# A linear-attention and state-space block on one core: chunk 14, the last v product and the passage to the output stage in another order, and slope rows padded to 64

## The chip, the core and the metric

The kernel runs on one core of one Trainium2 chip. The time is device microseconds (us) of one execution; the figure of a kernel is the median of its runs. One execution was also recorded by the hardware profiler, and all rows below come from it. The core's engines are TensorE (PE, with its weight loads as PEld), VectorE (DVE), ScalarE (ACT), GpSimd (POOL) and SyncE (SP, which here issues the DMAs). Each runs its own instructions in the order of the program and waits on semaphores of the others.

## The reference

Two branches over S = 2048 positions and D = 448 channels, mixed by a gate (shortened):

```python
g = sigmoid((x * gate_w).sum(-1, keepdims=True))
q, k, v = heads(x @ wqkv)                     # 16 heads of 28
phi = lambda t: where(t > 0, t + 1, exp(t)) + 1e-6
kv  = einsum("bhsd,bhse->bhde", phi(k), v);  z = phi(k).sum(s)
a   = (phi(q) @ kv) / (phi(q) . z + 1e-6) @ wo
K   = 2 Re sum_n C[d,n] exp(A[d,n] dt[d] l)   # kernel of the state-space branch, l = 0..L-1
b   = causal_conv(u, K) + u * D_skip
out = g * a + (1 - g) * b
```

## The kernel before

The positions are 16 chunks of 128. All products run on PE, single-precision data split into a rounded high part and a low part, so that a product takes three passes or so (names in h and l).

**The chunk loop** (`c` from 1 to 14) works on several chunks at once. In its turn c, PE computes k of chunk c+1 (`project`, tile `k`), the v products of chunks behind (`do_v`: `tri` times the scaled input, for the convolution's short part), q of chunk c (tile `q`), and adds chunk c to `g` (`do_g`), four banks that gather phi(k) against x. ACT and DVE make the features: `k_exp`, `k_max`, `k_high` (`pkh`), `k_low` (`pkl`), `k_sum` (adds phi(k) to `zb`), and likewise `q_exp`, `q_max`, `q_add` for `pq`. POOL takes low parts of x and the skip term. `v_post` scales the v product, `v_add` adds it to `y`, `v_row` sends its last row by DMA into `u`.

**The passage.** After the last k, `zb` is split into `zh` and `zl`, summed over partitions by a product with ones (tile `zo`, name `k`) and copied back to `zb`. `z_products` multiplies the rows of `u` by `ru` and sends `u` and `ru` by four DMAs into `zr`; `zst` is `zr` split into a high and a low part. `gate` and `gates_a` make the gate values of chunks 0 to 13, `gates_b` transposes them into `phs`, and `phi` sends these by DMA into `rows`. The banks of `g` are copied to `gs`, multiplied by `wv` (`kv_products`), masked and split into `kvz` (`kv_split`, `kv_again`), and multiplied by `wo` (split into `woh`, `wol`, in tiles `wos`) to `mh` and `ml` (`mrows`, products `m`). `inter(0)` and `inter(1)` multiply `gcat` by `zst` (products `z`) into `rc`, the carried state for chunks 0 to 7 and 8 to 15.

**The output stage** runs over c from 0 to 15. For each chunk: `norm_a` (POOL, `prod` = pq times zb), `norm_b` and `norm_d` (DVE, `den`: sums by head, plus 1e-6, times the gate's factor, reciprocal), `norm_c` (POOL, `pn` = pq times den), `norm_e` (ACT, copies 64 columns of `pn`), `turn` (PE, four transposes `tr`; then `th` on ACT and its low part on DVE), `tail` (ACT, gate rows into the low part), `attend` (PE, eleven products `a`), `final_b` (DVE, adds `y`, and the DMA out) and `final_c` (ACT). Each of these is issued some chunks ahead of `attend`. A generator `late` finishes q of chunk 15 and `inter(1)` within this loop.

**What sets the order.** The scheduling is manual: each engine executes in the order in which the code calls the helpers, so moving a call moves its instructions on their engine's queue. Tiles come from pools with a fixed number of buffers; a new tile waits until the readers of the old one are done. In the passage the helpers `z_products` (L539), `gates_b`, `turn`, `inter` and the calls from L634 to L927 are what the change touches.

Of the kernel before, what the change touches and what calls it, by code (L numbers as in the profile page):

```python
# [179 lines left out]
def gated_mix_kernel(ctx: ExitStack, tc: tile.TileContext, xin, wv_d, wo_d, abc_d, ldt_d, dsk_d,  # L180
# [82 lines left out]
    def low(eng, o, r, h):  # L263
        eng.tensor_tensor(out=o, in0=r, in1=h.bitcast(F32), op=ALU.subtract)  # L264
# [272 lines left out]
    U = slice(0, NC - 1)  # L537

    def z_products():  # L539
        zr = tp.tile([P, D], F32, name="zr", tag="w")[:64]  # L540
        POOL.memset(zr, 0.0)
        DVE.tensor_tensor(out=ru[U], in0=u[U], in1=ru[U], op=ALU.mult)
        for o in (0, 32):
            for k, w in enumerate((u[U], ru[U])):
                SP.dma_start(out=zr[o + k * (NC - 1):o + (k + 1) * (NC - 1)], in_=w)
        return zr
# [60 lines left out]
        q_max(n)  # L607
    do_g(0)
    woh, wol = [], []
    for c in range(1, NC - 1):  # L610
        if c == 1:
            load_x(4)
            gcr = tp.tile([P, D], F32, name="gcr", tag="w")[:KZ, :2 * RX].rearrange("p (g m) -> p g m", g=2)
            for o, i in ((mask, mask_d), (gcr, gcat_d), (sel, sel_d)):
                SP.dma_start(out=o, in_=i)
        elif c + 3 < NC:
            load_x(c + 3)
        if c == 4:
            SP.dma_start(out=wv, in_=wv_d)
            SP.dma_start(out=wo, in_=wo_d)  # L620
        ko, k_run = pieces(c + 1, wkh, wkl, D, "v0" if c in (2, 4) else "k")
        k_run(KA)
        if c == LAG + 2:
            steps(1)
        k_run(11)

        def split_next():
            if c + 2 < NC:
                split_x(c + 2)
                low(POOL, xl[c + 2], xr[c + 2][:, :NAT], xh[c + 2][:, :NAT])  # L630
# [36 lines left out]
        if c == 1:
            for n in range(2):
                q_add(n)
            steps(1)  # L670
        for n in now[1:]:
            v_post(n)
        if c == NC - 2:
            gate(0, NC - 2)
            g2 = gates_a(1, NC - 2)
        k_low(c + 1)
        k_sum(c + 1)
        for n in now[1:]:
            v_add(n)
        if c == NC - 2:  # L680
            zh = tp.tile([P, D], F32R, name="zh", tag="e")
            zl = tp.tile([P, D], F32R, name="zl", tag="t")
            ACT.copy(zh, zb)
            low(DVE, zl, zb, zh)
            zr = z_products()
        if c < NC - 2:
            vq = [vs.pop(0) for _ in range(1 + (c + 1 in TWICE))] if c > LAG + 1 else []
        if LAG + 2 < c < NC - 2:
# [12 lines left out]
        if LAG + 1 < c < NC - 2:  # L701
            for n in vq:
                do_w2(n)
        for n in now:
            v_row(n)
        if c > 1:
            q_add(c)
        drip(c, 2)
        if c in (NC - 6, NC - 4):
            wos = xs.tile([DJ, 2, 2, D], F32R, name="wos", tag="x")  # L710
            woh.append(wos[:, 0])
            wol.append(wos[:, 1])
            ACT.copy(woh[-1], wo[:, 2 * len(woh) - 2:2 * len(woh)])
        if c == NC - 6:
            low(POOL, wol[0], wo[:, 0:2], woh[0])
        if c < NC - 2:
            do_g(c)
        if c == LAG:
            POOL.tensor_copy(gcat, gcr)
# [33 lines left out]
    def norm_e(c):  # L753
        ACT.copy(pn[c][:, D:], pn[c][:, EV:D])
# [109 lines left out]
    v_post(vq[0])
    low(DVE, wol[1], wo[:, 2:4], woh[1])
    zo = ps.tile([P, 512], F32, name="k", tag="k")
    do_g(NC - 2, (0, 1, 2))
    PE.matmul(zo[:1, D:D + 1], lhsT=ones[:DJ, :1], rhs=oks, start=True, stop=True)
    PE.matmul(zo[:, :D], lhsT=ones_r, rhs=zh, start=True, stop=False)
    PE.matmul(zo[:, :D], lhsT=ones_r, rhs=zl, start=False, stop=True)  # L870
    ACT.copy(zb, zo[:, :D])  # L871
    DVE.tensor_copy(okn, zo[:1, D:D + 1])
# [126 lines left out]
def _layout(inputs):  # L999
# [79 lines left out]
```

## Time and profile before

| | |
|---|---|
| median of 3 runs | 183.65 us (183.55 to 183.81) |
| the profiled execution | 183.66 us, its span 181.9 us |
| PE, PEld | 175.4 us (96%), 155.1 us (85%) |
| DVE, ACT, POOL | 134.7 us (74%), 119.1 us (65%), 97.0 us (53%) |
| granted TensorE clock | 1.000 |

The span is from the first to the last instruction. The busy time of an engine is the union of its instructions; matmuls overlap each other, so PE's share says that it had work, and PE's waits show as distances between starts. In rows of the time order the columns are start, length (both us), engine, line, operation, tiles written and read, shape and count; in brackets stands how long the engine sat idle before it and who ended that. The loop's last turn (14) takes PE from about 111 to 118 us, the passage runs from there to 134 us, and the output stage from there to the end.

### The profile page before, as it was taken

To read this page: it belongs to the slowest core of one execution; us is meant where nothing else is said; L and a number is where in the kernel's file an instruction comes from. 1 tells how busy PE (TensorE), PEld (TensorE's weight loads), DVE (VectorE), ACT (ScalarE), POOL (GpSimd) and SP (SyncE) were. 2 spreads that over 40 slices of the span, in tenths; PEclk is the share of its full clock that TensorE was granted. 3 is DMA by queue.
4 is the path that set the end of the run, shared out by engine and by line. 5 is a ranking of instruction groups with operands and counts; after the bars stand their busy time and mean duration, and the time that the engine had idled before them with its cause. 6 is when DMAs were issued, how large, how long until landed. Compare 5 with 4: busy or idle time off the path is not lost.

```text
span 181.9 us, 2800 instructions
## 1 busy us (share of the span) xinstructions
PE 175.4 (96%) x896; PEld 155.1 (85%) x896; DVE 134.7 (74%) x265; ACT 119.1 (65%) x257; POOL 97.0 (53%) x90
## 2 busy tenths in 40 slices
PE   7999999999999999999999999999999999999991
PEld 7699999998988888898887999879887899889990
DVE  0876288765977799888978878577999698977530
ACT  3979596684755667666687676483665766765631
POOL 1059979651096437155284738039857857874000
PEclk9999999999999999999999999999999999999999
DMA  5999960960021302303032100000001212212212
GB/s 184 368 334 314 302 221 15 392 205 4 0 67 49 116 14 102 115 5 116 9 109 66 58 0 1 6 15 8 2 1 51 106 51 102 97 56 109 101 78 86
DMA packets 8356, 18.34 MB, mean 101 GB/s; under 512 B 1772, under 2 KB 5568, under 8 KB 8112
## 3 DMA queue, kind: packets, MB, share of 16 engines
q1 hardware_dynamic: 8192, 17.88, 28.9%
q10 hardware_dynamic: 144, 0.23, 0.4%
q8 instruction: 9, 0.15, 0.3%
q14 instruction: 11, 0.09, 0.2%
HBM read 14.25 MB, written 3.67 MB: 99 GB/s over the span
## 4 chain that ended last, share of the span: by engine, by line
PE 59%; DVE 15%; issue 11%; ACT 6%; POOL 5%; DMA 2%; POOLq 0%; ACTq 0%
PE a L800 16%; PE g L490 11%; PE q L391 10%; PE k L391 9%; PE tr L778 3%; PE v L391 2%; PE v L506 2%; PE v L556 2%; DVE den L734 2%; DMA xr<-in 2%; DVE v L497 2%; ACT xw L271 2%; POOL xw L264 1%; DVE th L783 1%; DVE wkl L264 1%
## 5 line engine op out<-in xcount | busy, mean ns | idle before, releaser
L264 POOL TENSOR_TENSOR xw<-xr,xw 128x448 fp32r<-128x448 f32 (+1 forms) x28 | 34.5, 1252 | 37.5 <-ACT xw L271 28.0
L490 PE MATMUL g<-pkh,xw 128*128 128x448 f32 x112 | 35.5, 366 | 0.0
L391 PE MATMUL q<-wqh,xw 128*128 128x450 f32 x112 | 32.4, 369 | 0.0
L391 PE MATMUL k<-wkh,xw 128*128 128x448 f32 x96 | 27.6, 369 | 0.0
L800 PE MATMUL a<-wkh,th 128*128 128x448 f32 (+1 forms) x119 | 26.9, 365 | 0.0
L729 POOL TENSOR_TENSOR prod<-pq,zb 128x448 f32<-128x448 f32 x16 | 19.2, 1204 | 10.9 <-ACT zb L871 8.3
L490 PE MATMUL g<-pkl,xw 128*128 128x448 f32 x64 | 23.5, 367 | 0.0
L490 PEld LDWEIGHTS g<-pkh,xw 128*128 128x128 f32 x112 | 21.1, 188 | 2.6
L391 PEld LDWEIGHTS q<-wqh,xw 128*128 128x128 f32 x112 | 21.0, 188 | 1.8
L800 PEld LDWEIGHTS a<-wkh,th 128*128 128x128 f32 x119 | 20.7, 191 | 1.2
L750 POOL TENSOR_TENSOR pn<-pq,den 128x448 f32<-128x448 f32 x16 | 15.5, 969 | 8.7 <-DVE den L741 4.4
L391 PEld LDWEIGHTS k<-wkh,xw 128*128 128x128 f32 x96 | 18.0, 188 | 2.0 <-issue 0.3
L278 POOL TENSOR_TENSOR y<-xr,rows 128x448 f32<-128x448 f32 x15 | 17.5, 1166 | 0.0
L391 PE MATMUL q<-wql,xw 128*128 128x450 f32 x42 | 15.4, 368 | 0.0
L805 DVE SCALAR_TENSOR_TENSOR ot<-y,og,a 128x448 f32<-128x448 f32 (+1 forms) x17 | 10.5, 618 | 6.4 <-PE a L800 6.4
L458 ACT ACTIVATE pq<-q 128x448 f32<-128x448 f32 x13 | 7.1, 544 | 12.2 <-DVE q L454 11.0
L412 DVE SCALAR_TENSOR_TENSOR k<-k,e 128x448 f32<-128x448 f32 x13 | 8.2, 632 | 9.0 <-ACT e L409 9.0
L271 ACT CAST xw<-xr 128x1024 fp32r<-128x1024 f32 x13 | 13.6, 1042 | 1.7 <-PE v L506 1.7
L782 ACT CAST th<-tr 128x512 fp32r<-128x512 f32 x16 | 9.4, 587 | 8.0 <-PE tr L778 7.7
L783 DVE TENSOR_TENSOR th<-tr,th 128x512 fp32r<-128x512 f32 x16 | 11.0, 689 | 4.3 <-ACT th L782 4.2
L811 ACT COPY pq<-a 128x448 f32<-128x448 f32 (+1 forms) x17 | 8.7, 514 | 6.9 <-DVE ot L805 6.8
L391 PE MATMUL k<-wkl,xw 128*128 128x448 f32 x36 | 13.2, 367 | 0.0
(182 smaller groups left out, 372.8 us busy)
## 6 DMA issues: line engine op xcount, KB each, us to landing
xr<-in SPq DMA_DIRECT2D x13, 512.0 KB, 4.9
out<-ot SPq DMA_DIRECT2D x15, 224.0 KB, 1.9
pq<-in SPq DMA_DIRECT2D x2, 896.0 KB
xr<-in SPq DMA_DIRECT2D x4, 256.0 KB
y<-in SPq DMA_DIRECT2D x4, 225.0 KB
wv<-in SPq DMA_DIRECT2D x1, 896.0 KB
wo<-in SPq DMA_DIRECT2D x1, 784.0 KB
y<-in SPq DMA_DIRECT2D x3, 224.0 KB, 4.3
```

What stands on the lines that cost most here:

```text
L264: eng.tensor_tensor(out=o, in0=r, in1=h.bitcast(F32), op=ALU.subtract)
L271: ACT.copy(h[:, :XC], r)
L278: POOL.tensor_tensor(out=y[:, c], in0=xr[c][:, NAT:LO], in1=dsk, op=ALU.mult)
L391: PE.matmul(o[:, :n], lhsT=a, rhs=b, start=run.n == 1, stop=not seq)
L490: PE.matmul(g[i][:a.shape[1], :D], lhsT=a, rhs=b, start=c == 0 and n == 0, stop=c == NC - 1 and n == len(seq) - 1)
L729: POOL.tensor_tensor(out=pd[c], in0=pq[:, c], in1=zb, op=ALU.mult)
L750: POOL.tensor_tensor(out=hd(n[:, :D]), in0=hd(pq[:, c]), in1=dn[c // 2][:, c % 2, :, None].to_broadcast([P, H, DH]), op=ALU.mult)
L782: ACT.copy(h, ov)
L783: DVE.tensor_tensor(out=l, in0=ov, in1=h.bitcast(F32), op=ALU.subtract)
L800: PE.matmul(a[:, lo:hi], lhsT=u_, rhs=w_[:, lo:hi], start=n == 0, stop=n == 10)
L805: DVE.scalar_tensor_tensor(out=ot[:, lo:hi], in0=y[:, c, lo:hi], scalar=og[:, c:c + 1], in1=a[:, lo:hi], op0=ALU.mult, op1=ALU.add)
L811: ACT.copy(pq[:, c, lo:hi], a[:, lo:hi])
```

## The change

The loop ends after c = 13, and turn 14 is written out behind it, in another order. In it DVE makes `ru` and scales the last v product ahead of the k maximum of chunk 15, the sum `k_sum` comes directly behind the maximum, and the gates come behind `zl`; the copy of `zb` comes ahead of `q_add`. The low parts of `wo` go to POOL, in halves of 448 columns. `zr`, `zst` and `gcat` have 94 rows instead of 62: the low part starts at row 64 instead of 32. POOL makes both parts of `zst`, behind its first two `prod`. Chunk 0 is transposed (`turn(0)`, and `norm_e(0)` before it on ACT) ahead of the rest of q of chunk 15 and of `mrows`. The last `v_add` moves from the passage into `late`, behind `attend(2)`. No instruction's result is dropped.

```diff
-KZ = 32 + NZ
+KZ = 64 + NZ
@@ z_products
-        zr = tp.tile([P, D], F32, name="zr", tag="w")[:64]
+        zr = tp.tile([P, D], F32, name="zr", tag="w")[:KZ]
-        for o in (0, 32):
+        for o in (0, 64):
-    for c in range(1, NC - 1):
+    for c in range(1, NC - 2):
...
-            low(POOL, wol[0], wo[:, 0:2], woh[0])
+            for j in range(2):
+                low(POOL, wol[0][:, j], wo[:, j], woh[0][:, j])
...
+    ko = project(NC - 1, wkh, wkl, D, "k")
+    kvz = xs.tile([DJ, 2, EV + NAT], F32R, name="kvz", tag="x")
+    POOL.memset(kvz.bitcast(F32), 0.0)
+    k_exp(NC - 1, ko)
+    do_v(NC - 1)
+    zr = z_products()
+    v_post(NC - 1)
+    for j in range(2):
+        low(POOL, wol[1][:, j], wo[:, 2 + j], woh[1][:, j])
+    POOL.memset(rows[DT:RX, :RG * P], 0.0)
+    k_max(NC - 1)
+    k_sum(NC - 1)
+    k_high(NC - 1)
...
+    ACT.copy(zh, zb)
+    k_low(NC - 1)
+    low(DVE, zl, zb, zh)
+    q_exp(NC - 2, project(NC - 2, wqh, wql, D + 2, "q"))
+    gate(0, NC - 2)
+    g2 = gates_a(1, NC - 2)
...
+    ACT.copy(zb, zo[:, :D])
+    q_max(NC - 2)
+    q_add(NC - 2)
...
     norm_a(0)
     norm_a(1)
-    POOL.memset(rows[DT:RX, :RG * P], 0.0)
-    do_g(NC - 2, (3,))
+    POOL.tensor_copy(zst, zr)
+    low(POOL, zst[64:], zr[64:], zst[64:])
     norm_bd(0)
     norm_c(0)
...
-            phs_low = gates_b(g2, "pkl")
-    ACT.copy(zst, zr[:KZ])
+            gates_b(g2, "pkl")()
+    norm_bd(1)
+    norm_a(2)
+    norm_c(1)
     norm_a(3)
+    norm_e(0)
...
     kv_again()
-    low(DVE, zst[32:], zr[32:KZ], zst[32:])
-    phs_low()
+    turn(0)
...
     mrows(1, p3, "a")
-    norm_bd(3)
+    norm_d(3, 1)
     norm_a(4)
-    v_add(vq.pop(0))
...
     def late():
         yield 2
+        v_add(c)
         last = inter(1)
```

What this does to the queues is seen at three places. The first is DVE from the k maximum (`k<-k,e`) of chunk 15 to the scaling of the last v product (`t<-v,rows`); `e_60` is the gate's row `e1`, `g_1243` the gate values to be transposed. Before:

```order
L412 SCALAR_TENSOR_TENSOR k<-k,e 128x448
L469 TENSOR_SCALAR e_60<-e_60 128x14
L470 RECIPROCAL og<-e_60 128x14
L471 TENSOR_SCALAR og<-og 128x14
L475 COPY g_1243<-og 128x13
L476 TENSOR_SCALAR g_1243<-og,sel 128x13
L427 SCALAR_TENSOR_TENSOR pkl<-k,pkh 128x448
L423 SCALAR_TENSOR_TENSOR zb<-k,zb 128x448
L264 TENSOR_TENSOR zl<-zb,zh 128x448
L542 TENSOR_TENSOR ru<-pq,ru 15x448
L454 SCALAR_TENSOR_TENSOR q<-q,e 128x448
L512 TENSOR_TENSOR t<-v,rows 128x448
```

The same stretch of DVE after the change:

```order
L542 TENSOR_TENSOR ru<-pq,ru 15x448
L512 TENSOR_TENSOR t<-v,rows 128x448
L412 SCALAR_TENSOR_TENSOR k<-k,e 128x448
L423 SCALAR_TENSOR_TENSOR zb<-k,zb 128x448
L427 SCALAR_TENSOR_TENSOR pkl<-k,pkh 128x448
L264 TENSOR_TENSOR zl<-zb,zh 128x448
L469 TENSOR_SCALAR e_60<-e_60 128x14
L470 RECIPROCAL og<-e_60 128x14
L471 TENSOR_SCALAR og<-og 128x14
L475 COPY g_1279<-og 128x13
L476 TENSOR_SCALAR g_1279<-og,sel 128x13
L454 SCALAR_TENSOR_TENSOR q<-q,e 128x448
```

`ru` and `t` now stand ahead of the maximum, the sum `zb` directly behind it, and the five gate operations behind `zl`.

The second place is POOL from the memset of `kvz` to `pn` of chunk 1. Before:

```order
L640 MEMSET kvz 112x1792
L541 MEMSET zr 64x448
L729 TENSOR_TENSOR prod<-pq,zb 128x448 x2
L875 MEMSET rows 48x1024
L750 TENSOR_TENSOR pn<-pq,den 128x448
L729 TENSOR_TENSOR prod<-pq,zb 128x448
L750 TENSOR_TENSOR pn<-pq,den 128x448
```

POOL after the change:

```order
L709 MEMSET kvz 112x1792
L541 MEMSET zr 94x448
L264 TENSOR_TENSOR wos<-wo,wos 112x448 x2
L716 MEMSET rows 48x1024
L747 TENSOR_TENSOR prod<-pq,zb 128x448 x2
L884 CAST zst<-zr 94x448
L264 TENSOR_TENSOR zst<-zr,zst 30x448
L768 TENSOR_TENSOR pn<-pq,den 128x448
L747 TENSOR_TENSOR prod<-pq,zb 128x448
L768 TENSOR_TENSOR pn<-pq,den 128x448
```

The two halves of the last `wo` split and the `rows` memset stand ahead of the first `prod`, and the two `zst` operations between the first two `prod` and the first `pn`.

The third place is ACT from the last copy `gs` to the first `th`. Before:

```order
L884 COPY gs_1279<-g_143 128x448
L887 CAST zst<-zr 62x448
L831 CAST kvz<-k 112x2x112
L831 CAST kvz<-tr 112x2x112
L835 CAST kvz<-kvz 112x2x64
L858 CAST wkh<-m_1388 128x448
L754 COPY pn<-pn 128x64 x2
L858 CAST wkh<-m_1399 128x448
L843 CAST zs_1407<-z_1405 48x448
L782 CAST th<-tr 128x512
```

ACT after the change:

```order
L890 COPY gs_1302<-g_143 128x448
L772 COPY pn<-pn 128x64
L849 CAST kvz<-k 112x2x112
L849 CAST kvz<-tr 112x2x112
L853 CAST kvz<-kvz 112x2x64
L800 CAST th<-tr 128x512
L876 CAST wkh<-m_1399 128x448
L772 COPY pn<-pn 128x64
L876 CAST wkh<-m_1409 128x448
L861 CAST zs_1417<-z_1415 48x448
```

The copy into `pn` of chunk 0 now stands ahead of the casts of `kvz`, and `th` of chunk 0 ahead of the first `m`. On PE the four transposes of chunk 0 move from behind the first `z` to directly behind the products on `gs`; nothing else on PE changes place.

More of the change, by code (lines that the diff above doesn't have):

```diff
@@ L637, in gated_mix_kernel @@
         drip(c, 0)
-        if c == NC - 2:
-            kvz = xs.tile([DJ, 2, EV + NAT], F32R, name="kvz", tag="x")
-            POOL.memset(kvz.bitcast(F32), 0.0)
         k_exp(c + 1, ko)
@@ L652, in gated_mix_kernel @@
             do_v(n)
-        if c == NC - 2:
-            now = []
         for n in now[:1]:
@@ L672, in gated_mix_kernel @@
             v_post(n)
-        if c == NC - 2:
-            gate(0, NC - 2)
-            g2 = gates_a(1, NC - 2)
         k_low(c + 1)
@@ L679, in gated_mix_kernel @@
             v_add(n)
[L680 to L686, printed above, removed]
+        if c:
             vq = [vs.pop(0) for _ in range(1 + (c + 1 in TWICE))] if c > LAG + 1 else []
-        if LAG + 2 < c < NC - 2:
+        if c > LAG + 2:
             for n in vq:
@@ L700, in gated_mix_kernel @@
                 do_w1(n)
-        if LAG + 1 < c < NC - 2:
+        if c > LAG + 1:
             for n in vq:
@@ L714, in gated_mix_kernel @@
         if c == NC - 6:
-            low(POOL, wol[0], wo[:, 0:2], woh[0])
-        if c < NC - 2:
-            do_g(c)
+            for j in range(2):
+                low(POOL, wol[0][:, j], wo[:, j], woh[0][:, j])
+        do_g(c)
         if c == LAG:
             POOL.tensor_copy(gcat, gcr)
+    ko = project(NC - 1, wkh, wkl, D, "k")
[11 more added lines that the diff above has]
+    k_high(NC - 1)
+    zh = tp.tile([P, D], F32R, name="zh", tag="e")
+    zl = tp.tile([P, D], F32R, name="zl", tag="t")
+    ACT.copy(zh, zb)
[4 more added lines that the diff above has]
+    g2 = gates_a(1, NC - 2)
+    zo = ps.tile([P, 512], F32, name="k", tag="k")
+    do_g(NC - 2, (0, 1, 2))
+    PE.matmul(zo[:1, D:D + 1], lhsT=ones[:DJ, :1], rhs=oks, start=True, stop=True)
+    PE.matmul(zo[:, :D], lhsT=ones_r, rhs=zh, start=True, stop=False)
+    PE.matmul(zo[:, :D], lhsT=ones_r, rhs=zl, start=False, stop=True)
+    ACT.copy(zb, zo[:, :D])
+    q_max(NC - 2)
+    q_add(NC - 2)
+    DVE.tensor_copy(okn, zo[:1, D:D + 1])
+    do_g(NC - 2, (3,))
     gs = [xp.tile([P, 2, D], F32, name="gs%d" % i, tag="xr") for i in range(2)]
@@ L862, in mrows @@
             low(DVE, mh[64:, t], o[64:, :D], mh[64:, t])
[L864 to L872, printed above, removed]
     norm_a(0)
     norm_a(1)
-    POOL.memset(rows[DT:RX, :RG * P], 0.0)
-    do_g(NC - 2, (3,))
+    POOL.tensor_copy(zst, zr)
+    low(POOL, zst[64:], zr[64:], zst[64:])
     norm_bd(0)
     norm_c(0)
-    norm_bd(1)
-    norm_a(2)
-    norm_c(1)
     for i in range(4):
@@ L903, in gated_mix_kernel @@
     mrows(2, ps, "v0")
-    norm_e(0)
     norm_e(1)
@@ L907, in gated_mix_kernel @@
     last = inter(0)
-    turn(0)
     last()
     mrows(0, p3, "a")
+    norm_b(3)
     mrows(1, p3, "a")
-    norm_bd(3)
+    norm_d(3, 1)
     norm_a(4)
-    v_add(vq.pop(0))
     ACT.copy(rc[0][:DT], mh[:DT, 3].bitcast(F32))
     q_run(QA[2])
+    norm_e(2)
     turn(1)
-    norm_e(2)
     norm_a(5)
@@ L1039, in _layout @@
     gcat = np.zeros((KZ, 2, RX))
-    gcat[:NZ, :, DT:] = gcat[32:, :, DT:] = gc
+    gcat[:NZ, :, DT:] = gcat[64:, :, DT:] = gc
     sel = np.zeros((P, 2))
```

## Prediction

> **What bounds the kernel now.** I read the page's engine shares first.
>
> ```profile
> PE 175.4 (96%) x896; PEld 155.1 (85%) x896; DVE 134.7 (74%) x265; ACT 119.1 (65%) x257; POOL 97.0 (53%) x90
> ```
>
> PE is busy 96% of the span, so an edit gains only what shortens PE's work or a place where PE waits. Next I read PE's own order of time through the passage (start, length, group), looking at distances between starts, since lengths overlap.
>
> ```profile
> 118.45 0.47 PE L869 MATMUL k<-zh,ones_r 128*128 128x448 f32 x1
> 119.04 0.48 PE L870 MATMUL k<-zl,ones_r 128*128 128x448 f32 x1
> 119.36 0.36 PE L490 MATMUL g<-pkl,xw 128*64 128x448 f32 x1
> ...
> 122.52 1.83 PE L820 MATMUL k<-gs,wv 128*112 128x112 f32 x16
> 124.19 1.74 PE L820 MATMUL tr<-gs,wv 128*112 128x112 f32 x16
> 125.69 0.45 PE L391 MATMUL q<-wql,xw 128*128 128x450 f32 x1
> ...
> 126.59 2.01 PE L857 MATMUL m<-wos,kvz 112*128 112x448 f32 x9
> 128.63 0.46 PE L842 MATMUL z<-zst,gcat 62*112 62x448 f32 x1
> ...
> 129.43 2.69 PE L857 MATMUL m<-wos,kvz 112*128 112x448 f32 x12
> ...
> 133.42 0.90 PE L778 MATMUL tr<-ident,pn 128*128 128x128 f32 x4
> 134.07 1.68 PE L800 MATMUL a<-wkh,th 128*128 128x448 f32 x7
> ...
> 135.80 0.78 PE L800 MATMUL a<-wkl,th 128*128 128x448 f32 x3
> ...
> 136.96 1.68 PE L800 MATMUL a<-wkh,th 128*128 128x448 f32 x7
> ...
> 138.69 0.77 PE L800 MATMUL a<-wkl,th 128*128 128x448 f32 x3
> 139.63 0.90 PE L778 MATMUL tr<-ident,pn 128*128 128x128 f32 x4 [0.17 <-POOL pn L750]
> 140.28 1.68 PE L800 MATMUL a<-wkh,th 128*128 128x448 f32 x7
> ...
> 142.01 0.78 PE L800 MATMUL a<-wkl,th 128*128 128x448 f32 x3
> 142.72 0.46 PE L842 MATMUL z<-zst,gcat 62*112 62x448 f32 x1
> 143.10 0.66 PE L778 MATMUL tr<-ident,pn 128*128 128x128 f32 x4
> 143.52 1.65 PE L800 MATMUL a<-wkh,th 128*128 128x448 f32 x7
> ...
> 145.21 0.77 PE L800 MATMUL a<-wkl,th 128*128 128x448 f32 x3
> 145.82 0.60 PE L778 MATMUL tr<-ident,pn 128*128 128x128 f32 x4
> 146.17 1.68 PE L800 MATMUL a<-wkh,th 128*128 128x448 f32 x7
> ```
>
> The last three rows are an undisturbed chunk of the output stage: 145.21 to 145.82 is three products, so 0.205 each; four transposes take 0.35 to 146.17, and the whole step from three products to the next seven is 0.96. Against these floors PE loses:
> - 0.385 before the product of `zl` (0.59 less 0.205) and 0.115 behind it: **0.50**.
> - In the first 16 products on `gs`: 1.67 to the next sixteen. The second sixteen take 1.50, and 0.08 of the difference is only that the product behind them starts early and runs longer (0.45, where others last 0.36): **0.09**.
> - Around the first slope product `z`: nine products to `z` 2.04 against 1.85 (nine times 0.205), then 0.80 to the next `m` against 0.56: **0.43**.
> - In the transposes of chunk 2: 0.65 against 0.35: **0.30**. Of chunk 3: 1.16 against 0.96: **0.20**. Of chunk 4: 1.59 against 0.96: **0.63**.
> - Around the second `z`: 1.51 against 0.96 and 0.205: **0.35**.
>
> Together 2.50 us. Who ends these waits is seen on the other engines and in the chain:
>
> ```profile
> 115.14 0.63 DVE L412 SCALAR_TENSOR_TENSOR k<-k,e 128x448 f32<-128x448 f32 x1 [2.12 <-ACT e L409]
> 117.77 0.57 ACT L683 CAST zh<-zb 128x448 fp32r<-128x448 f32 x1 [1.41 <-DVE zb L423]
> 118.36 0.63 DVE L264 TENSOR_TENSOR zl<-zb,zh 128x448 fp32r<-128x448 f32 x1 [0.63 <-ACT zh L683]
> 121.19 2.58 POOL L729 TENSOR_TENSOR prod<-pq,zb 128x448 f32<-128x448 f32 x2 [8.31 <-ACT zb L871]
> ```
>
> ```profile
> 122.71 0.63 DVE den L734
> ...
> 127.34 0.95 DVE zst L264
> ...
> 134.40 1.22 DVE y L520
> ...
> 138.63 0.95 POOL pn L750
> ```
>
> `zl` ends at 118.99 and its product starts at 119.04. The other waits are the end of one string: `zb`, POOL's first product at 121.19, then DVE almost without a pause from 122.71 to the `pn` that PE awaits at 139.63. Two pieces of that string, 0.95 and 1.22, are no part of the normalisation.
>
> **The change, part by part.**
>
> *Sum of k first.* DVE sat idle 2.12 before the k maximum of chunk 15, and then ran five small gate operations ahead of the sum. In the new order `ru` and the last v product fill that idle time (two operations of about 0.6), the sum follows the maximum at once, and the gates come behind `zl`. From 115.14: maximum 0.63, sum to 116.4; the rounded part `pkh` and `zh` on ACT, at 0.57 each, to 117.5; `zl` 0.63, to 118.2. PE comes to it at 118.45 + 0.205 = 118.66: 0.50 goes. Behind that, `zb` is copied ahead of chunk 14's q features: product end 119.14 (118.66 and 0.48), copy 0.57 like `zh`, POOL's first product at 119.7, where it was 121.19. The copies `gs` wait for no q any more either, and PE meets them 0.5 earlier, as they come: I count the 0.09 as gone.
>
> *Slope rows.* The split of `zst` moves from ACT and DVE to POOL, behind POOL's first two products; the `wo` split of the last half goes from DVE to POOL at about 112.9, where it idled till 121.19; the `rows` memset moves there too. The prices, from the view of groups (busy us, mean ns of one):
>
> ```profile
> L264 POOL TENSOR_TENSOR xw<-xr,xw 128x448 fp32r<-128x448 f32 x15 | 17.8, 1183 | 1.8 <-issue 1.8
> L264 POOL TENSOR_TENSOR wos<-wo,wos 112x896 fp32r<-112x896 f32 x1 | 2.1, 2143 | 4.0 <-ACT wos L713 4.0
> L287 POOL CAST wqh<-y 128x450 fp32r<-128x450 f32 x1 | 1.0, 1016 | 8.2 <-DMA y<-in 8.2
> L719 POOL CAST gcat<-gcr 62x224 fp32r<-62x224 f32 x1 | 0.4, 370 | 0.0
> L754 ACT COPY pn<-pn 128x64 f32<-128x64 f32 x16 | 3.8, 246 | 0.3
> ```
>
> The cast of 94x448 lies between 0.37 (half the columns) and 1.02 (450); twice 0.37 is 0.74, I take 0.75. The low part is one 448-column operation, 1.18. So POOL: 119.7 + 2.58 + 0.75 + 1.18 = 124.2, then `pn` of chunk 0 (0.95, from the chain) to 125.2, and its 64-column copy on ACT (0.25) to 125.4. PE now transposes chunk 0 right behind the `gs` products, which end at 125.69 - 0.59 = 125.1; the fourth transpose, which needs that copy, is due 0.33 later at 125.43. It fits by nothing, so I charge **0.10**; ends are 0 (cast 0.37, products 1.18 each) and 0.5 (cast 1.02, low part as slow as 1.4).
>
> *What is queued behind that copy.* ACT takes the chunk-0 copy before the two casts of `kvz`. They begin at 125.4; each is half the columns of the 0.57 and 0.63 operations above, so the high part of the first half is there at 125.8 and its low part at 126.2. PE asks for the high part after four pieces of q, at 125.1 + 0.10 + 0.35 + 0.82 = 126.4, for the low one 0.8 later. Cost nothing, cover 0.6; if the copy is later by more, PE waits that much at `m`. On POOL, `prod` and `pn` of chunks 1 to 3 follow from 125.2.
>
> *The z products.* The wait of the first for `zst` goes, since POOL has it at 124.2 and PE comes past 128. Both still show 0.35 of another kind: the second waited for nobody and yet PE took 0.71 to reach it and 0.38 to leave it, where 0.61 and 0.205 are normal. The row with 112 partitions shows none of this (`m`: nine last 2.01, which is eight steps of 0.205 and a length of 0.37), the one with 62 does. The change contracts over 94. Ends: as 62 (nothing gained, 0.35 twice) and as 112 (all gained); 94 is nearer to 112, I take all. The Trainium skill, TensorEngine Tiling (Array Packing), section Key Properties, says that changing the tiling mode drains the engine, and its modes hold 32, 64 or 128 rows; by it 94 rows would count as 128 and the gain is whole, without it the sum would stand 0.7 higher. The 0.38 agrees with a drain.
>
> *DVE relieved.* Of the string above the 0.95 (`zst`) leaves DVE and the 1.22 (last v added to `y`) moves behind chunk 2's products; the gate-row low part goes ahead of the string. It enters the `kvz` part at much the same moment as before (125.4), so the `den` that fed 138.63 comes 2.2 earlier, at 136.4, and `pn` of chunk 4 at 137.4. PE, 1.4 earlier by then (0.50 + 0.09 + 0.43 + 0.30 + 0.20, less 0.10, from 138.69 + 0.61 = 139.30), wants it at 137.9. So 0.30, 0.20 and 0.63 go, with 0.5 to spare. Next to be late: `y` is added between chunk 2 and the second `z`; the slope row's copy on ACT uses the tile that the addition frees, so it waits for it. At an undisturbed 0.63 that ends with `z` itself; cost nothing, at most 0.6.
>
> *POOL in the loop.* At chunk 10 one 896-column operation becomes two of 448: 2 x 1.183 against 2.143, 0.22 more at most, on a queue whose results DVE uses a chunk later. I charge **0.10** (ends 0 and 0.22). The longer transfers into `zr` and the 94-row constants ride on queues with nobody waiting: free, covered until POOL's cast at 122.3.
>
> **Sum.** 2.50 - 0.10 - 0.10 = 2.30. The profiled execution took 183.66 (span 181.9 and 1.8 around it), 0.01 over the median of the runs: 183.66 - 2.30 = **181.4**.
>
> **Rivals.**
> - *Ninety-four rows cost what 62 do.* For it: no row of 94 exists. 181.4 + 0.7 = 182.1.
> - *POOL holds up chunk 0.* The upper prices above: 181.9.
> - *DVE locked out by POOL.*
>
> ```profile
> 113.79 0.92 SPq L545 DMA_DIRECT2D zr<-pq  x1
> ...
> 133.99 1.15 POOL L729 TENSOR_TENSOR prod<-pq,zb 128x448 f32<-128x448 f32 x1 [2.16 <-DVE den L734]
> ...
> 134.32 1.30 DVE L520 TENSOR_TENSOR y<-y,t 128x448 f32<-128x448 f32 x1
> ```
>
>   `y<-y,t` and `zl` both read two tiles of SBUF; `zl` took 0.63 with POOL idle, `y<-y,t` 1.30, ending 0.5 after POOL's `prod` did (135.14). `ru` too reads two, and now stands before the k maximum while POOL splits `wo`. If it arrives just as the second half starts, it loses 1.18, the maximum comes about 1 late and `zl` at 119.2: the 0.50 stays, 181.9. Against it: the halves start near 112.9 and 114.0, and the transfer at 113.79, which waits for the same rows of `u`, shows that they are there by then, so `ru` waits for the first half alone. The Trainium skill, SBUF — State Buffer, section Who interferes with whom, has this as a rule: a VectorE instruction with two SBUF inputs and a GpSimd one that reads SBUF exclude each other for a whole instruction. The 1.30 agrees; by it the rival is a matter of 0.2 us of timing.
> - *The DVE string still binds*, as `den` of chunks 3 to 5 are not early enough: 1.1 stays, 182.5.
> - *Slower.* POOL's two `zst` operations hold `pn` of chunk 0; ACT, in order, holds both `kvz` casts behind it, and every DVE step of the string after them. Beyond 125.4 each us costs one, so from 127.7 on the change loses; at 128.5 it would be 184.4. That needs 3 us more on POOL than the 1.93 I count; the longest POOL operation quoted is 2.14 for twice the columns.
>
> **Chances.** Forecast 0.58 (own range 181.1 to 181.7); 94 rows 0.13; POOL late 0.10; DVE locked out 0.07; string binds 0.06; slower 0.05; 0.01 for no effect. The range reaches from 180.9, where the 0.10s fall away and a small wait more, to 182.5, where 94 rows and most of a late POOL come together or the string still binds. 0.2% (0.37 us) is about what a measurement of this kernel can tell: faster 0.91, same 0.04, slower 0.05.
>
> **What would show it.** PE after: `zl`'s product 0.2 behind `zh`'s; the first `prod` at 119.7; transposes of chunk 0 directly behind the `gs` products with at most 0.1 lost; `z` to the next group about 0.2 instead of 0.38; no `pn` wait before chunks 3 and 4; the second `z` at 140.6 to 140.8 instead of 142.72, and the same distance from there to the end. I am wrong if the k maximum starts past 115.6, if `pn` of chunk 0 ends past 125.7, or if a `z` still takes 0.38.

## The result, and the profile after

The changed kernel takes 182.12 us (median of 14 runs), the kernel before 183.81 in the same comparison: ratio 0.9916, 95% interval 0.989 to 0.9943. It is faster by 1.69, about three quarters of the 2.30 that the forecast (181.4) subtracts. The profiled execution took 182.32, with a span of 180.5, against 183.66 and 181.9 before.

The engine shares first (busy us, share of the span, instructions):

```profile
PE 174.0 (96%) x896; PEld 155.1 (86%) x896; DVE 133.9 (74%) x263; ACT 118.9 (66%) x256; POOL 99.8 (55%) x95
```

PE's busy time fell by 1.4, the span by as much, with as many products: what went away is time by which waiting had lengthened PE's records. PE through the passage and the first chunks of the output stage (start, length, group):

```profile
118.36 0.37 PE L490 MATMUL g<-pkh,xw 128*128 128x448 f32 x1
118.91 0.19 PE L730 MATMUL k<-oks,ones_r 112*1 112x1 f32 x2 [0.18 <-DVE pkl L427]
...
119.44 0.47 PE L732 MATMUL k<-zl,ones_r 128*128 128x448 f32 x1
119.75 0.36 PE L490 MATMUL g<-pkl,xw 128*64 128x448 f32 x1
...
122.89 1.83 PE L838 MATMUL k<-gs,wv 128*112 128x112 f32 x16
124.56 1.74 PE L838 MATMUL tr<-gs,wv 128*112 128x112 f32 x16
126.13 0.60 PE L796 MATMUL tr<-ident,pn 128*128 128x128 f32 x4
...
127.40 1.99 PE L875 MATMUL m<-wos,kvz 112*128 112x448 f32 x9
129.23 0.37 PE L860 MATMUL z<-zst,gcat 94*112 94x448 f32 x1
129.44 2.64 PE L875 MATMUL m<-wos,kvz 112*128 112x448 f32 x12
...
133.39 0.60 PE L796 MATMUL tr<-ident,pn 128*128 128x128 f32 x4
133.75 1.67 PE L818 MATMUL a<-wkh,th 128*128 128x448 f32 x7
...
138.77 0.60 PE L796 MATMUL tr<-ident,pn 128*128 128x128 f32 x4
139.13 1.67 PE L818 MATMUL a<-wkh,th 128*128 128x448 f32 x7
...
141.45 0.36 PE L860 MATMUL z<-zst,gcat 94*112 94x448 f32 x1
141.66 0.60 PE L796 MATMUL tr<-ident,pn 128*128 128x128 f32 x4
```

Both `z` products now start one ordinary step behind the product ahead and are left after 0.21. The transposes of chunks 2 to 4 take 0.35 or 0.36. The place that did not improve is the first: from the last `g` product to the first product with ones (`k<-oks`) 0.55, on to `zl` 0.53, and 0.31 behind it. Where nothing waits (the run e5 below) the same steps are 0.30, 0.43 and 0.21, so 0.45 is lost here (0.94 against 1.39). Why is on DVE and POOL:

```profile
114.19 1.70 DVE L542 TENSOR_TENSOR ru<-pq,ru 15x448 f32<-15x448 f32 x1 [0.87 <-DMA pq<-ut]
116.35 0.61 DVE L412 SCALAR_TENSOR_TENSOR k<-k,e 128x448 f32<-128x448 f32 x1
118.77 0.61 DVE L264 TENSOR_TENSOR zl<-zb,zh 128x448 fp32r<-128x448 f32 x1
```

```profile
113.14 2.26 POOL L264 TENSOR_TENSOR wos<-wo,wos 112x448 fp32r<-112x448 f32 x2
120.62 2.31 POOL L747 TENSOR_TENSOR prod<-pq,zb 128x448 f32<-128x448 f32 x2 [3.13 <-ACT zb L733]
```

`ru` is 15 rows of work and takes 1.70: it comes while POOL is in the two `wo` halves (113.14 to 115.40) and ends 0.49 behind the second, which began at 114.25 (115.40 less the 1.15 of one half), 0.06 after `ru`. The k maximum, forecast at 115.14, starts at 116.35, `zl` ends at 119.38 instead of 118.2, and `prod` starts at 120.62, not 119.7.

### The profile page after: what moved, and what is told of

The parts are those of the page before. It is cut to its first block, busy times and chain, and to the rows that moved or that the text cites. A ratio compares the mean times of both kernels' runs of the same rounds, so it can differ in the third digit from the quotient of the medians.

```text
span 180.5 us, 2801 instructions
## 1 busy us (share of the span) xinstructions
PE 174.0 (96%) x896; PEld 155.1 (86%) x896; DVE 133.9 (74%) x263; ACT 118.9 (66%) x256; POOL 99.8 (55%) x95
## 4 chain that ended last, share of the span: by engine, by line
PE 72%; DVE 11%; ACT 8%; DMA 3%; issue 3%; SPq 0%; DVEq 0%
PE a L818 20%; PE g L490 13%; PE q L391 11%; PE k L391 9%; PE tr L796 4%; DMA y<-in 3%; PE v L506 3%; PE v L391 3%; PE m L875 2%; DVE v L497 2%; PE v L556 2%; DVE k L412 2%; DVE zb L423 2%; ACT xw L271 2%; ACT pkh L420 2%
## 5 line engine op out<-in xcount | busy, mean ns | idle before, releaser
L747 POOL TENSOR_TENSOR prod<-pq,zb 128x448 f32<-128x448 f32 x16 | 18.6, 1165 | 4.0 <-ACT zb L733 3.1
L420 ACT ACTIVATE pkh<-k 128x448 fp32r<-128x448 f32 x13 | 7.1, 544 | 9.9 <-DVE k L412 7.7
L497 DVE SCALAR_TENSOR_TENSOR v<-xw,rows 128x448 f32<-128x448 f32 x16 | 10.8, 704 | 3.3 <-ACT ru L372 2.1
```

The lines of the kernel that those rows point to most:

```text
L420: ACT.add(pkh[c], pks[c], 1e-6)
L497: DVE.scalar_tensor_tensor(out=v, in0=xh[c][:, NAT:LO].bitcast(F32), scalar=-1.0, in1=slope, op0=ALU.mult, op1=ALU.mult)
L747: POOL.tensor_tensor(out=pd[c], in0=pq[:, c], in1=zb, op=ALU.mult)
```

## Experiments

The four theories: *lock* (`ru` waits for POOL's `wo` halves, and the missing 0.50 is this wait; the expectations call what the two engines can't use at once the port), *drain* (a product over 62 rows costs PE a gap on both sides, one over 94 does not), *string* (the waits at chunks 2 to 4 came from DVE, because of `zst` and the late `v_add`), and its rival *order* (they came from the order of the output stage).

The first `v<-w` product on PE starts between 47.58 us (e9) and 49.89 us (e8) in the profiled executions, and nearly all edits lie behind it. So beside the medians the table gives one stretch of each profiled execution: from the start of that product to the end of PE's last product. It comes from one execution per kernel; how well such stretches repeat is seen where no edit reaches: from the transposes of chunk 8 to the end it is 26.62 to 26.70 in all fourteen. For before and after it follows from these rows (177.37 + 0.50 - 47.66 = 130.21; 176.03 + 0.50 - 47.89 = 128.64):

```profile
47.66 0.37 PE L506 MATMUL v<-w,tri 128*128 128x448 f32 x1
...
177.37 0.50 PE L800 MATMUL a<-wkl,th 128*128 128x224 f32 x3
```

```profile
47.89 0.36 PE L506 MATMUL v<-w,tri 128*128 128x448 f32 x1
...
176.03 0.50 PE L818 MATMUL a<-wkl,th 128*128 128x224 f32 x3
```

| kernel | median us | ratio to before, 95% | stretch us | less the stretch of after |
|---|---|---|---|---|
| before | 183.65 to 184.12 | | 130.21 | +1.57 |
| after | 182.12 | 0.9916 (0.989 to 0.9943) | 128.64 | |
| e1 halves apart | 182.26 | 0.9945 (0.9914 to 0.9976) | 128.56 | -0.08 |
| e2 wo on DVE | 182.30 | 0.9919 (0.989 to 0.9948) | 128.88 | +0.24 |
| e3 62 rows | 182.88 | 0.995 (0.9918 to 0.9982) | 129.22 | +0.58 |
| e4 v_add in the passage | 182.65 | 0.9941 (0.9919 to 0.9963) | 128.92 | +0.28 |
| e5 wo behind t | 181.76 | 0.9876 (0.9837 to 0.9915) | 128.18 | -0.46 |
| e6 quarters | 182.92 | 0.9938 (0.9908 to 0.9968) | 129.00 | +0.36 |
| e7 padding alone | 184.14 | 1.0005 (0.9973 to 1.0038) | 130.00 | +1.36 |
| e8 zst on ACT and DVE | 182.78 | 0.9911 (0.9875 to 0.9947) | 128.66 | +0.02 |
| e9 zst and v_add back | 182.69 | 0.995 (0.9917 to 0.9982) | 129.20 | +0.56 |
| e10 output order undone | 182.50 | 0.9912 (0.9873 to 0.995) | 129.12 | +0.48 |
| e11 no wo split on POOL in the loop | 181.29 | 0.9876 (0.9836 to 0.9917) | 127.65 | -0.99 |
| e12 gap between the halves | 182.03 | 0.9901 (0.9869 to 0.9934) | 128.18 | -0.46 |

The intervals of the ratios, 0.4 to 0.8% wide, tell few of these kernels apart; the stretches and the single waits do, and they carry the verdicts below.

### The lock: where POOL's wo halves stand

**e1**: one half ahead of the `zr` memset, the other behind it.

```diff
+    low(POOL, wol[1][:, 0], wo[:, 2], woh[1][:, 0])
     # behind do_v, ahead of z_products (which holds the zr memset)
...
-    for j in range(2):
-        low(POOL, wol[1][:, j], wo[:, 2 + j], woh[1][:, j])
+    low(POOL, wol[1][:, 1], wo[:, 3], woh[1][:, 1])
```

> The changed kernel with one thing moved: POOL's two wo halves are parted, one ahead of the memset of zr and one behind it, so that POOL only writes when ru arrives. In the changed kernel ru took 1.70 us and the k maximum of chunk 15 started at 116.35. Theory A (POOL locks DVE out: ru waits for both halves): ru takes about 0.6, the maximum starts at 115.5, the zl product stands 0.2 behind the zh product, the ones product no longer waits; 0.5 us less than the changed kernel (182.1), so 181.6, ratio to the kernel before 0.989. Theory B (ru is late because its rows land late, or the wait at the ones product has another cause): ru stays long or the wait stays, 182.1, ratio 0.9916.

Measured: no gain. In this kernel's timeline, DVE and then POOL:

```profile
113.91 1.71 DVE L542 TENSOR_TENSOR ru<-pq,ru 15x448 f32<-15x448 f32 x1 [0.86 <-DMA pq<-ut]
```

```profile
113.99 1.15 POOL L264 TENSOR_TENSOR wos<-wo,wos 112x448 fp32r<-112x448 f32 x1
```

The attempt missed its aim, since the second half again began just when `ru` came. It shows that `ru` loses even where it starts 0.08 ahead of the half, and for a single half (1.71).

**e2**: the last `wo` split back on DVE, behind `okn`.

```diff
-    for j in range(2):
-        low(POOL, wol[1][:, j], wo[:, 2 + j], woh[1][:, j])
...
     DVE.tensor_copy(okn, zo[:1, D:D + 1])
+    low(DVE, wol[1], wo[:, 2:4], woh[1])
```

> The changed kernel with the last wo low part back on DVE, behind okn, as one operation of 896 columns; POOL has nothing that reads while ru runs. Theory A: ru about 0.6 and the wait at the ones product gone (0.5 less), but the first prod on POOL is now shut out by the wo operation (1.5 instead of 1.18) and the string behind it starts up to 0.4 later; PE has room for part of that: 181.6 to 181.9. Theory B: 182.1 or up to 0.4 more.

```profile
114.05 0.61 DVE L542 TENSOR_TENSOR ru<-pq,ru 15x448 f32<-15x448 f32 x1 [0.87 <-DMA pq<-ut]
...
119.98 1.07 DVE L264 TENSOR_TENSOR wos<-wo,wos 112x896 fp32r<-112x896 f32 x1
```

```profile
120.02 3.15 POOL L746 TENSOR_TENSOR prod<-pq,zb 128x448 f32<-128x448 f32 x2 [3.75 <-ACT zb L731]
```

```profile
125.98 0.66 PE L795 MATMUL tr<-ident,pn 128*128 128x128 f32 x4 [0.25 <-POOL pn L767]
```

`ru` takes 0.61 and the wait at `zl` is gone, as the lock says. The gain is given back 6 us later, more of it than expected: DVE's split (119.98 to 121.05) now shuts out POOL's `prod`, 3.15 instead of 2.31, and PE waits for `pn` of chunk 0, 0.41 of it at this place (1.98 from the second sixteen to the transposes, against 1.57).

**e5**: both halves on POOL, held back by a memset of 8 columns that waits for `t`, which follows `ru`.

```diff
+    POOL.memset(rows[DT:RX, :8], 0.0)
     for j in range(2):
         low(POOL, wol[1][:, j], wo[:, 2 + j], woh[1][:, j])
-    POOL.memset(rows[DT:RX, :RG * P], 0.0)
+    POOL.memset(rows[DT:RX, 8:RG * P], 0.0)
```

> One edit against the changed kernel: a memset of 8 columns of rows, which has to wait for the last v_post (t), stands on POOL ahead of the two wo halves, and the rest of the rows memset behind them; so no POOL operation that reads SBUF runs or is about to start when ru comes. Theory A (ru is locked out by the wo halves, and the 0.50 at the zl product hangs on this alone): ru takes 0.61 again, k max comes at about 115.3, the wo halves run 115.2 to 117.5 beside DVE operations that have one operand in PSUM, end ahead of zl, the PE wait of about 0.5 at zh and zl goes as in the run with wo on DVE, and here nothing is given back, since prod has POOL to itself: 181.5 to 181.7, ratio to the kernel before 0.988 to 0.989. Rival 1: the halves now shut out zb, pkl or zl instead (any DVE operation collides, not only those with both operands in SBUF): zl not before 118.5, 182.0 to 182.3. Rival 2: the 0.5 is given back at the next place, as with wo on DVE (turn(0) or the masks of chunk 0 wait): 182.1.

PE, POOL and DVE of this run:

```profile
118.23 0.37 PE L490 MATMUL g<-pkh,xw 128*128 128x448 f32 x1
118.53 0.19 PE L731 MATMUL k<-oks,ones_r 112*1 112x1 f32 x2
...
118.96 0.37 PE L733 MATMUL k<-zl,ones_r 128*128 128x448 f32 x1
119.17 0.37 PE L490 MATMUL g<-pkl,xw 128*64 128x448 f32 x1
```

```profile
115.56 2.27 POOL L264 TENSOR_TENSOR wos<-wo,wos 112x448 fp32r<-112x448 f32 x2
```

```profile
114.11 0.61 DVE L542 TENSOR_TENSOR ru<-pq,ru 15x448 f32<-15x448 f32 x1 [0.86 <-DMA pq<-ut]
...
117.24 0.63 DVE L427 SCALAR_TENSOR_TENSOR pkl<-k,pkh 128x448 fp32r<-128x448 f32 x1 [0.61 <-ACT pkh L420]
```

The wait is gone and nothing is given back: 0.46 off the stretch, 181.76. The halves now lie beside `zb` (116.00) and `pkl`, which take their usual 0.62; one of their inputs, `k`, is in PSUM. Beside the halves it is the operation with both inputs in SBUF that loses. The Trainium skill, SBUF — State Buffer, section Who interferes with whom, draws the line there too; the 1.70 against these 0.62 agrees. There is another kind of loss in this run: the gate's `e<-e` (L469, one SBUF input), elsewhere 0.17, took 0.55 and ended 0.03 behind POOL's `rows` memset (117.89 to 118.83), which only writes. In e12 it took 0.17 and the stretch is the same, so it cost nothing here.

**e6** (the halves as four quarters in the old place) and **e12** (halves apart, the `t` memset between them) ask how long the lock holds.

```diff
# e6
-    for j in range(2):
-        low(POOL, wol[1][:, j], wo[:, 2 + j], woh[1][:, j])
+    for j in range(4):
+        f = slice(j % 2 * D // 2, (j % 2 + 1) * D // 2)
+        low(POOL, wol[1][:, j // 2, f], wo[:, 2 + j // 2, f], woh[1][:, j // 2, f])
# e12
+    low(POOL, wol[1][:, 0], wo[:, 2], woh[1][:, 0])
+    POOL.memset(rows[DT:RX, :8], 0.0)
+    low(POOL, wol[1][:, 1], wo[:, 3], woh[1][:, 1])
+    POOL.memset(rows[DT:RX, 8:RG * P], 0.0)
```

> The two wo halves on POOL as four quarters of 224 columns, at the same place as in the changed kernel. Which of two locks it is: if POOL keeps the port for as long as its next operation stands ready (what the run with the halves apart suggests), ru again waits for all four, ends at 115.8 to 116.1 and takes 1.6 to 2.0, and the time stays at 182.1 to 182.4. If DVE gets the port at the end of the POOL operation that runs when it asks, ru waits for the rest of one quarter only, takes 0.7 to 1.2, k max comes at about 115.4 to 115.9, and half or more of the 0.5 at the zl product is gained: 181.6 to 181.9.

> One edit against the changed kernel: between the two wo halves on POOL stands the memset of 8 columns of rows, which waits for t behind ru; so the first half runs where it did, the second only when ru and t are through, and POOL stands idle when the first half ends. Theory A' (POOL keeps the port as long as its next reading operation is ready behind the running one): the first half ends at about 114.3, and with nothing behind it ru, which comes at 114.1 to 114.2, waits for its rest alone: it takes 0.65 to 0.9, k max starts at 115.4 to 115.6, as the prediction's step had it, and 0.3 to 0.5 of the wait at zh and zl goes: 181.6 to 181.9. Rival (DVE waits for more than the running operation whatever follows): ru takes 1.2 or more, and the wait stays: 182.1.

First e6, then e12, each DVE and POOL:

```profile
115.86 2.00 DVE L542 TENSOR_TENSOR ru<-pq,ru 15x448 f32<-15x448 f32 x1 [0.86 <-DMA pq<-ut]
```

```profile
114.84 2.55 POOL L264 TENSOR_TENSOR wos<-wo,wos 112x224 fp32r<-112x224 f32 x4
```

```profile
114.01 0.61 DVE L542 TENSOR_TENSOR ru<-pq,ru 15x448 f32<-15x448 f32 x1 [0.86 <-DMA pq<-ut]
```

```profile
112.98 1.15 POOL L264 TENSOR_TENSOR wos<-wo,wos 112x448 fp32r<-112x448 f32 x1
```

In e6 `ru` comes 1.02 into the quarters, in the second of four (each about 0.64), and ends 0.47 behind the last: it let two operations pass that began after it (116.10 and 116.73). So here the row of POOL operations counted, not only the one that ran; the stretch is 0.36 longer than that of the changed kernel. This rests on e6 alone. In e12 `ru` comes 0.12 before the end of a half with nothing behind it and loses nothing. That doesn't tell a row from a single operation: `ru` ends 0.47 to 0.49 behind POOL's last operation where it waits and takes 0.61 alone, so, as an estimate, it needs the port only some 0.13 after its recorded start, when this half was over. For the same reason the changed kernel's loss needs no row: its second half ran by then. What e12 shows is the cause of the loss: its 0.46 equals that of e5, which puts the whole effect on the second half. Both medians (182.92 and 182.03) lie above what was expected, which the stretches don't show to this extent.

### The drain: e3 and e7

**e3**: the changed kernel with the low slope rows from row 32 again. **e7**: the kernel before with the padding alone. The edit, as in e3 (the constant `gcat` goes along; e7 makes it the other way round in the kernel before, where DVE has the low part):

```diff
-KZ = 64 + NZ
+KZ = 32 + NZ
...
-        for o in (0, 64):
+        for o in (0, 32):
...
-    low(POOL, zst[64:], zr[64:], zst[64:])
+    low(POOL, zst[32:], zr[32:KZ], zst[32:])
```

> The changed kernel with the slope rows back at 62 (low part from row 32), all else as changed. Theory C (the products z over 62 rows make PE stop on both sides): the step from the products before z over z and the transposes grows from 0.96 + 0.2 to about 1.5, at both z, 0.3 to 0.35 each; 0.6 to 0.7 more than the changed kernel: 182.8, ratio 0.995. Rival D (in the kernel before, PE waited there for data and the rows do not matter): both z as in the changed kernel, 182.1.

> The kernel before with the padding alone (the low part of the slope rows from row 64, so that the two z products have 94 rows instead of 62); nothing is moved. Theory C (the 62-row product costs a drain of some 0.3 at each of two places, and 94 rows cost none): both z products lose their gap, and the time falls by 0.5 to 0.75 to 183.1 to 183.3, ratio 0.996 to 0.9973. Rival: the gaps stood in the shadow of a DVE wait that comes right behind (the transposes wait for DVE in any case), and 0.35 or less is seen: 183.45 to 183.8.

PE in e3, then in e7:

```profile
127.19 1.99 PE L875 MATMUL m<-wos,kvz 112*128 112x448 f32 x9
129.11 0.46 PE L860 MATMUL z<-zst,gcat 62*112 62x448 f32 x1
129.50 0.67 PE L875 MATMUL m<-wos,kvz 112*128 112x448 f32 x2
```

```profile
127.25 2.01 PE L857 MATMUL m<-wos,kvz 112*128 112x448 f32 x9
129.29 0.46 PE L842 MATMUL z<-zst,gcat 94*112 94x448 f32 x1
129.59 0.60 PE L778 MATMUL tr<-ident,pn 128*128 128x128 f32 x4
```

In e3 nobody is waited for, yet the 62-row product is reached 0.09 late and left after 0.39 instead of 0.21, and the `m` behind it lose another 0.06: from the first of the nine to the q behind the last `m` it is 4.84 (127.19 to 132.03), in the changed kernel 4.51 (127.40 to 131.91). From the three products ahead of the second `z` to the seven behind it, it is 1.50 against 1.17. So the 62 rows cost 0.33 at each place, close to the 0.35 of the forecast; the stretch shows 0.58, mainly because the transposes of chunks 6 and 7 lose 0.12 less than in the changed kernel. In e7 the gap goes too, but only 0.21 of it reaches the end (130.21 to 130.00), and the median shows nothing (ratio 1.0005): the first `z` still comes 0.19 late, waiting for `zst`, and the wait at the transposes of chunk 3 grows from 0.20 to 0.36. Expected were 0.5 to 0.75, so the rival was right. The padding pays in full only where the work behind it is ready, as in the changed kernel.

### String or order: e4, e8, e9, e10

All four are the changed kernel with one thing put back: e4 the `v_add` into the passage's DVE string, e8 the `zst` pair onto ACT and DVE, e9 both, e10 the order of the output stage.

```diff
# e4
     norm_a(4)
+    v_add(NC - 1)
...
-        v_add(c)
# e8 (e9 is e4 and e8 together)
-    POOL.tensor_copy(zst, zr)
-    low(POOL, zst[64:], zr[64:], zst[64:])
...
+    ACT.copy(zst, zr)
...
     kv_again()
+    low(DVE, zst[64:], zr[64:], zst[64:])
# e10: turn(0) and norm_e(0) behind mrows(2) and inter(0), norm_bd(3) in one piece, and
-    norm_e(2)
     turn(1)
+    norm_e(2)
```

> The changed kernel with the last addition of v to y back in the passage, ahead of the slope row's copy, where it reads two SBUF tiles while POOL works. Theory E (the DVE string decides the waits before chunks 2 to 4): the addition takes 0.6 to 1.3 there, den of chunks 4 and 5 and pn of chunk 4 come that much later (pn of chunk 4 had 0.6 us to spare before PE asked for it), PE waits 0.1 to 0.7 before chunk 4: 182.2 to 182.8. Rival F (other parts of the change made all the room): no wait returns, 182.1, or 0.15 less because the addition no longer stands ahead of the second slope row.

> The changed kernel with the two zst operations back where they were before (cast on ACT behind the gs copies, low part on DVE behind kv_again); all else as changed. Theory D (the gain at the transposes of chunks 2 to 4, 1.13 in the prediction, comes from the DVE string being shorter by zst low and v_add, of which v_add alone was worth 0.18): some 0.5 to 0.9 of PE waits comes back at the transposes of chunks 1 to 4, 182.6 to 183.0. Rival: the gain there is that of the order (chunk 0 turned earlier, POOL started earlier) and the zst operations have slack on either engine: 182.0 to 182.2, or a little faster, since POOL then reaches chunk 0 1.7 earlier.

> The changed kernel with both pieces back in the DVE string of chunks 0 to 4: the zst pair on ACT and DVE, and the last v added to y ahead of chunk 3. All else as changed. Either alone cost PE 0 (zst) and 0.18 (v_add) at the transposes. Theory F (one string with about 0.5 of slack: whichever piece comes back first is covered, the second is not): DVE is 0.62 and 0.63 or more later, less the slack of about 0.5, so PE waits 0.6 to 0.9 in all before the transposes of chunks 2 to 4; with v_add gone from the later place some 0.16 comes back there: 182.6 to 182.9. Rival (the pieces do not add, the gain is that of the order of the normalisation): 0.2 or less at the transposes, 182.1 to 182.3.

> The changed kernel with the order of the output stage as before: turn(0) and the copy of chunk 0 behind the products of rows 0, the den of chunk 3 in one piece behind the last mrows, the copy of chunk 2 behind turn(1); the zst pair stays on POOL, the last v_add in its late place, the passage as changed. Theory F (the waits at chunks 2 to 4 are those of a DVE string that carried two pieces too many; the order is worth little): at most 0.3 comes back, 182.1 to 182.4. Rival (the order is what removed them): 0.6 to 1.1 of waits come back at the transposes of chunks 1 to 4, 182.7 to 183.2.

PE at chunk 4 in e9, and at chunk 2 in e10 with ACT behind it:

```profile
137.95 0.78 PE L818 MATMUL a<-wkl,th 128*128 128x448 f32 x3
138.73 0.90 PE L796 MATMUL tr<-ident,pn 128*128 128x128 f32 x4
139.38 1.68 PE L818 MATMUL a<-wkh,th 128*128 128x448 f32 x7
```

```profile
133.25 0.90 PE L796 MATMUL tr<-ident,pn 128*128 128x128 f32 x4
133.91 1.68 PE L818 MATMUL a<-wkh,th 128*128 128x448 f32 x7
```

```profile
133.03 0.59 ACT L800 CAST th<-tr 128x512 fp32r<-128x512 f32 x1
133.52 0.24 ACT L772 COPY pn<-pn 128x64 f32<-128x64 f32 x1
```

e8 costs nothing (+0.02), against an expected 0.5 to 0.9; its median of 182.78 would fit that, but in its comparison the kernel before took 184.08, and the ratio is nearly that of the changed kernel. e4 costs 0.28, 0.24 of it at chunk 4. Both together cost 0.47 there (138.73 to 139.38 and 0.17 ahead, against 0.35), more than the sum of the two, as a string with slack has it, though less than the 0.6 to 0.9 expected. e10 brings back 0.31 at chunk 2, the wait of before (0.65 from group to group there, 0.66 here): the last transpose needs ACT's 64-column copy, and that stands behind the 0.59 cast of `turn(1)`. The rest of e10's 0.48 is spread in steps below 0.1. In the kernel before the rows say the same: `pn` of chunk 2 was through POOL at 130.70, its copy ran on ACT only at 133.69, behind the cast from 133.21. So the two theories share the waits: chunk 2 was order on ACT, and of chunk 4's 0.63 the DVE string is shown for 0.47; the rest is open.

Chunk 3's 0.20 came back in none of these runs. In the kernel before its copy (136.58) stood behind `tail` (136.26), which waited for DVE's `th`, and that came behind the `y<-y,t` of 1.30; this points at the DVE string too, but no run shows it. At all three chunks the products `a` start 0.13 or 0.14 behind the end of ACT's copy (133.94, 136.82 and 140.14), so what holds this copy is the question to ask at each.

### The loop: e11

e5, and the first two `wo` halves as one DVE operation each behind the `w` of two chunks, where DVE idles.

```diff
-        if c == NC - 6:
-            for j in range(2):
-                low(POOL, wol[0][:, j], wo[:, j], woh[0][:, j])
...
+        if c in (NC - 5, NC - 4):
+            j = c - NC + 5
+            low(DVE, wol[0][:, j], wo[:, j], woh[0][:, j])
```

> The run with the last wo halves behind t, and the first two wo halves taken off POOL in the loop as well: each is one DVE operation of 448 columns (0.6) behind the w of chunks 12 and 13, where DVE waits 0.77 to 0.83 for PE's v. Theory A carried to the loop: there the wo halves on POOL push the x split and with it the y product of POOL about 2.2 later, onto DVE's v (both operands in SBUF), which takes 1.38 instead of 0.6, so PE waits 0.50 for the v product of chunk 12. Without them v takes 0.6, the wait falls to 0 to 0.2, and nothing else moves: 0.3 to 0.5 less than the run with the halves behind t, so 181.2 to 181.5, ratio to the kernel before 0.9855 to 0.987. Rival: the DVE halves do not fit the idle time and push the k maximum, and a wait of 0.2 to 0.6 comes up at the next g or k products: 181.7 to 182.0.

POOL in the changed kernel, DVE there, and DVE in e11:

```profile
91.82 2.28 POOL L264 TENSOR_TENSOR wos<-wo,wos 112x448 fp32r<-112x448 f32 x2 [3.97 <-ACT wos L699]
...
96.42 1.15 POOL L278 TENSOR_TENSOR y<-xr,rows 128x448 f32<-128x448 f32 x1
```

```profile
96.68 1.38 DVE L497 SCALAR_TENSOR_TENSOR v<-xw,rows 128x448 f32<-128x448 f32 x1
```

```profile
96.41 0.63 DVE L497 SCALAR_TENSOR_TENSOR v<-xw,rows 128x448 f32<-128x448 f32 x1
```

The same lock stood in the loop all along (in the kernel before `v`, at 96.49, took 1.25 beside the `y` of 96.09): the `wo` split pushed `y<-xr,rows` onto DVE's `v`. Without it `y` starts at 94.86, `v` takes 0.63, the new half behind `w` 0.61 in DVE's idle time, PE's wait for the v product of chunk 12 is gone, and the stretch is 0.53 shorter than in e5. At 181.29 it has the lowest median of the study; its ratio to the kernel before equals that of e5, so the 0.53 rests on the stretch.

## Why the prediction was right or wrong

The direction and two thirds of the sum were right (1.57 of the 2.30 in the stretch); the time came out 0.7 above the forecast. It lies inside the range of 180.9 to 182.5, and that is partly luck: the upper part of the range stood for 94 rows that cost what 62 do, a late POOL or a binding string, and none of these came. The rival with the right mechanism was priced at 181.9; 182.1 was the price of the rival on the 94 rows, which e3 refutes.

- **Sum of k first: the step that failed.** It counted 0.50 as gone, and let `ru` wait "for the first half alone". The order of starts that it estimated was right: the transfer of the rows of `u` went out at 114.09, `ru` started at 114.19, the second half at 114.25. What failed is the assumption that being ahead by so little is enough: `ru` waited for the second half too, the k maximum started at 116.35, past the 115.6 that was to show the prediction wrong, and the 0.50 became a loss of 0.07 (from the last `g` product to the one behind `zl`: 1.32 before, from 118.04 to 119.36, and 1.39 after). This was the rival "DVE locked out", given 0.07 and priced at 181.9; its mechanism and place were right. e2, e5 and e12 show the term: with `ru` at 0.61 the wait goes, and this place takes 0.93 or 0.94. So there was 0.38 to gain and not 0.50: behind the `zh` product an undisturbed step is 0.31 in e5, and the floor taken was 0.205.
- **The 0.09 at the `gs` products** did not go (1.67 to the second sixteen, as before). It had been tied to the same 0.50; in e5 and e11 it is still there, so that link was wrong by itself. Its cause isn't known.
- **Slope rows.** Confirmed: 0.43 and 0.34 gone at the two places, 0.33 of each by the rows (e3) and the rest of the first by `zst` being in time. The 94-row cast took 0.57 where 0.75 was estimated. e8 shows that moving the pair to POOL was worth nothing here.
- **DVE relieved.** The 0.30, 0.20 and 0.63 went as forecast, but the reason, the DVE string, is shown for chunk 4 alone, and there for 0.47: chunk 2's 0.30 was ACT's order, which the working never looked at. A right number with a cause that was half wrong: at chunk 2 it was luck.
- **The 0.10 for chunk 0** wasn't needed: PE took up the transposes at 126.13 directly behind the second sixteen.
- **POOL in the loop**: charged 0.10, measured 0.11 (the wait ahead of chunk 12's v product rose from 0.38 to 0.49).
- **Not foreseen**: the transposes of chunks 6 and 7 lose 0.05 and 0.11, about 0.10 more than before. It stays in e9, where `v_add` is back in the passage, so the late `v_add` isn't its cause. By the rows it is ACT's copy again: `pn` of chunk 7 was through POOL at 145.39, its copy came at 147.18, behind `tail` (146.86) and `final_c` (146.30), which waited for DVE. In e3, where PE comes some 0.6 later, only 0.01 and 0.03 are lost.

Summed: 0.43 + 0.30 + 0.20 + 0.63 + 0.34 - 0.07 - 0.11 - 0.10 = 1.62, against 1.57 in the stretch.

## What to carry to other kernels

Before an operation is put on GpSimd, list the VectorE operations with both inputs in SBUF that can fall beside it, and price each at the end of the GpSimd operation that runs and, as the worst case, of the whole row that stands ready behind it. A start that is estimated to lie 0.1 or 0.2 us ahead can't exclude such a meeting; a small instruction that waits for the right event can. When several engines meet at one wait, undo one cause at a time: at chunks 2 and 4 the same kind of wait had two different owners.

## What the runs showed of the hardware

- `ru` waited for POOL operations that began after it: 1.70 where it started 0.06 ahead of the second of two halves, 1.71 where it started 0.08 ahead of a single one, 2.00 where it came in the second of four quarters and let the third and fourth pass. It lost nothing when a gap followed (0.61). Waiting for the whole row isn't the general rule: in the kernel before, `zst` on DVE (0.95 from 127.34) came in between a `pn` and a `prod` of POOL, and that `prod` took 1.53; and `y<-y,t` (1.30 from 134.32) came in behind a `prod`, ahead of a `pn` that took 1.33 instead of 0.94. What decides between these cases stays open.
- The recorded start of an operation is not the moment from which it shuts the other engine out: in e12 `ru` starts 0.12 ahead of the end of POOL's half and loses nothing, in e1 it starts 0.08 ahead of the beginning of one and loses 1.10.
- The 62-row product cost 0.33 a place beside products over 112 and 128 rows, the 94-row one nothing.
